# Products of two head pairs in one step, and six parts of w_out streamed from DRAM

## The chip, the core and the metric

The kernel runs on one core of a Trainium2 chip. A core has five engines with queues of their own: TensorE (PE, matrix products; its weight loads are shown as PEld), VectorE (DVE), ScalarE (ACT), GpSimd (POOL) and SyncE (SP), which here issues every DMA. Each works through its instructions in order and waits on semaphores of the others. The metric is the device time of one execution in microseconds; a profiled execution also gives the span from the first to the last instruction.

## What is computed

Eight batches with eight heads of attention over keys and values that are averaged in groups of eight, then a feed-forward layer with a squared ReLU over all 4608 tokens:

```python
B, H, S, D = 8, 8, 576, 64
k_p = k.reshape(B, H, S // 8, 8, D).mean(axis=3)      # 72 pooled keys a head
v_p = v.reshape(B, H, S // 8, 8, D).mean(axis=3)
scores = np.matmul(q, k_p.transpose(0, 1, 3, 2)) / np.sqrt(D)
attn = np.exp(scores - np.max(scores, axis=-1, keepdims=True))
attn = attn / (np.sum(attn, axis=-1, keepdims=True) + 1e-09)
x = np.matmul(attn, v_p).transpose(0, 2, 1, 3).reshape(B * S, H * D)   # 4608 x 512
h = np.maximum(x @ w_in, 0.0)                          # w_in 512 x 2048
out = h * h @ w_out                                    # w_out 2048 x 512
```

All is in float32. From chunk 1 on the two big products are made as three products of a high and a low half (float32r) each: high times high, high times low, low times high.

## The kernel before

The tokens are cut into 12 chunks of 384 (CH); a chunk spans one batch or two. For each chunk the 2048 hidden features are worked in 16 parts of 128 (NFC). One step of the main loop is one (chunk, part): `hidden` makes the part's hidden values on PE into one of two PSUM banks, ACT takes the ReLU, DVE squares it, ACT and DVE split it in a high half gh and a low half gl, and two steps later (LAG) `project` adds its product with that part of w_out to three PSUM banks that stay for the whole chunk. In PE's order a step is: `hidden` of this step, the small products that fall due, `project` of two steps before.

The attention of a chunk is made under the feed-forward layer of the chunk before. It goes by pairs of heads, p = 0 to 3, as stages spread over steps: `turn_q`, `split_q`, `scores`, `exponents`, `send_sums`, `fetch_sums`, `reciprocals`, `fetch_reciprocals`, `weigh_values`. STEADY gives, for chunk 2 on, each pair's first step relative to its chunk's start (-22, -18, -14, -10) and the stages' offsets from it (-1 to 8). So `weigh_values` of pairs 0 to 3 falls in steps -14, -10, -6 and -2, each pair in a step of its own. EARLY is the same for chunk 1, whose stages differ; chunk 0 is made in the prologue.

`weigh_values` (av): for each of the pair's two heads PE multiplies the pooled values vp by the exponents sc; the two heads' results stand in the upper and lower 64 partitions of one PSUM bank of tag "a" (three banks, used by the scores as well). These products are plain float32, of 64 output columns of PE; in the profile each is two passes, and the two heads' passes run side by side. DVE multiplies the bank by the reciprocals rb, ACT copies the high half xh, and DVE subtracts for the low half xl. `hidden` of the chunk reads xh and xl.

The sums over exponents travel through DRAM: SP sends them (rs), fetches them in another shape (rc), DVE takes reciprocals (rr), SP sends those (rd) and fetches them broadcast to all partitions (rb).

The order of all this is fixed by a table: `at(step, f, ...)` enters a stage for a step, and the main loop emits a step's stages in program order on every engine. Loads are collected during a step and issued by SP at its end, behind the small transfers that the stages issue themselves.

Weights stay on the chip. Each of 32 parts (16 of w_in, 16 of w_out) is loaded raw (`land`), unpacked by ACT and DVE (`magnitude`, `to_float32`: tiles wf) and split in two halves (`split_weights`: tiles wt, named w_i and w_o in the profile). All these tiles, and most large tiles of the prologue (values and keys of batches 0 and 1, early exponents te), come from one pool of 4 KB tiles, tag "w", with 2 * NFC + 1 = 33 buffers. A tile gets the buffer of one that has been read for the last time, and its first writer waits for that reader. In the prologue POOL sums the values of batch 1 out of such tiles, heads 0 to 7 in order (`by_halves`; the tile v_1_6 holds heads 6 and 7).

Of the kernel before, what the change touches and what calls it, by code (L numbers as in the profile page):

```python
# [9 lines left out]
F32 = mybir.dt.float32  # L10
F32R = mybir.dt.float32r
# [3 lines left out]
ALU = mybir.AluOpType  # L15
# [22 lines left out]
def pooled_attn_relu2_ffn(  # L38
# [16 lines left out]
    PE, DVE, ACT, GP, SP = (InOrder(tc, e) for e in (nc.tensor, nc.vector, nc.scalar, nc.gpsimd, nc.sync))  # L55
# [4 lines left out]
    P = 128  # L60
    POOL = 8
    SP_ = S // POOL
    NPAIR = H // 2
    NFC = DFF // P
# [4 lines left out]
    NCH = NT // CH  # L69
# [4 lines left out]
    SCALE = 1.0 / (D ** 0.5) / POOL  # L74
    LAG, QL = 2, 5

    IDLE = (10, 3)
    STB, SCB, LD, OB = 1, 2, 4, 3


    FIRST, EAGER, AHEAD = 4, 10, 4
# [2 lines left out]
    SPLIT = 6  # L84


    STEADY = ((-22, -18, -14, -10), (-1, 0, 1, 3, 4, 5, 6, 7, 8))
    KV0 = -39
    EARLY = ((-16, -13, -10, -7), (0, 1, 2, 3, 5))

    NKT = H * SP_ // QT
    KV_AT = (("k", (0, 1, 2, 4, 5, 6), 9, 10, 12), ("v", (9, 10, 12, 13, 15, 16), 19, 20, None))
# [3 lines left out]
    wts = ctx.enter_context(tc.tile_pool(name="wts", bufs=1))  # L96
    sb = ctx.enter_context(tc.tile_pool(name="sb", bufs=2))
    dram = ctx.enter_context(tc.tile_pool(name="dram", bufs=3, space=bass.MemoryType.DRAM))
# [20 lines left out]
    def load(dst, src):  # L119
        loads.append((dst, src))  # L120

    def issue_loads():
        for dst, src in loads:
            dma(dst, src)
        loads.clear()

    def split(hi, lo, src, eng=None):
        ACT.copy(hi, src)
        (eng or DVE).tensor_tensor(lo, src, hi.bitcast(F32), op=ALU.subtract)
# [3 lines left out]
    raw, wf, wt = {}, {}, {}  # L133

    def w_tile(dt, name):
        return wts.tile([P, 2, 512], dt, name=name, tag="w", bufs=2 * NFC + 1)

    halves = {}

    def half_tile(kind, name):  # L140

        if kind not in halves:
            halves[kind] = w_tile(F32, name)
            return halves[kind][:, 0, :]
        return halves.pop(kind)[:, 1, :]
# [37 lines left out]
    def keep_busy(n):  # L183

        for i in range(0, n):
            if i % 8 == 0:
                t = ps_a.tile([P, 512], F32, name=f"idle_{n}_{i}", tag="a")
            PE.matmul(t[:, :P], lhsT=ident, rhs=ident, start=True, stop=True)
# [25 lines left out]
    def pool_k(b, i):  # L214
        if i % KT == 0:
            loaded["kp", b, i // KT] = sb.tile([QT, KT, 2, D], F32, name=f"kp_{b}_{i}", tag="kp", bufs=2)
        kp, kt = loaded["kp", b, i // KT][:, i % KT], loaded.pop(("k", b, i))
        if b == 1:
            by_halves(kp[:, 0, :], kt)
            GP.tensor_tensor(kp[:, 1, :], kt[:, :D], kt[:, D:2 * D], op=ALU.add)  # L220
        else:
            DVE.tensor_reduce(kp[:, 0, :], kt.rearrange("p (o d) -> p d o", d=D), axis=AX.X, op=ALU.add)
            DVE.tensor_copy(kp[:, 1, :], kp[:, 0, :])
# [99 lines left out]
    def segments(c):  # L323
        t, segs = c * CH, []
        while t < (c + 1) * CH:
            b = t // S
            n = min((b + 1) * S, (c + 1) * CH) - t
            segs.append((b, t - c * CH, n))
            t += n
        return segs  # L330
# [191 lines left out]
    def weigh_values(c, p):  # L522

        if p == 0 and c == 0:
            x0.extend(w_tile(F32, f"x_{c}_{i}")[:, :, :CH] for i in range(2))
        elif p == 0:
            xts[c] = (sb.tile([P, NPAIR, CH], F32R, name=f"xh_{c}", tag="xh", bufs=2),
                      sb.tile([P, NPAIR, CH], F32R, name=f"xl_{c}", tag="xl", bufs=2))
        sc, rb = live.pop((c, p))
        av = ps_a.tile([P, 512], F32, name=f"av_{c}_{p}", tag="a")  # L530
        for b, o, n in segments(c):
            for i in range(2):
                PE.matmul(av[i * D:(i + 1) * D, o:o + n], lhsT=kv[b][2][:, 2 * p + i, :], rhs=sc[:, i, o:o + n],
                                 start=True, stop=True)

        def then():
            if c == 0:
                ACT.copy(x0[p // 2][:, p % 2, :], av[:, :CH])
                return
            xh, xl = xts[c]  # L540
            if c == 1:
                split(xh[:, p, :], xl[:, p, :], av[:, :CH])
                return
            DVE.tensor_tensor(rb, av[:, :CH], rb, op=ALU.mult)
            split(xh[:, p, :], xl[:, p, :], rb)

        return then

    gts = {}

# [33 lines left out]
        split(gh, gl, gts[c, fc])  # L584
        gts[c, fc] = (gh, gl)

    accs = {}

    def project(c, fc):
        if fc == 0:  # L590
            accs[c] = [ps_o.tile([P, 512], F32, name=f"o_{c}_{t}", tag=f"o{t}") for t in range(NTT)]
        g, key = gts.pop((c, fc)), ("o", fc)
        for t in range(NTT):
            tt = slice(t * P, (t + 1) * P)
            if c == 0:
                prods = [(g[:, tt], wf[key])]
            else:
                prods = [(g[x][:, tt], wt[key][:, w, :]) for x, w in ((0, 0), (0, 1), (1, 0))]
            for i, (a, w) in enumerate(prods):
                PE.matmul(accs[c][t], lhsT=a, rhs=w, start=fc == 0 and i == 0, stop=fc == NFC - 1 and i == len(prods) - 1)  # L600

        def store():
            for t in range(NTT):
                ob = sb.tile([P, DM], F32, name=f"ob_{c}_{t}", tag="ob", bufs=OB)
                ACT.copy(ob, accs[c][t])
                dma(out[c * CH + t * P:c * CH + (t + 1) * P, :], ob)

        return store if fc == NFC - 1 else None
# [5 lines left out]
    def at(step, f, *a):  # L614
        work.setdefault(max(step, -PRO), []).append((f, a))
# [27 lines left out]
    issue_loads()  # L643
    keep_busy(IDLE[0])
    for i in range(KT + 2):
# [4 lines left out]
    pool_k(0, KT + 2)  # L650
    keep_busy(IDLE[1])
    after = [token_scores(0, 0), transpose_k(0, 1)]
# [15 lines left out]
    for p in range(NPAIR):  # L668
# [4 lines left out]
        if p > 1:  # L673
            keep_busy(IDLE[1])
        if p:
            weigh_values(0, p - 1)()
        if p:
            keep_busy(IDLE[1])
        if p in (1, 2):
# [5 lines left out]
    to_float32(*first_keys[2:])  # L685
    keep_busy(IDLE[1])
    weigh_values(0, NPAIR - 1)()
    keep_busy(IDLE[1])
    for hf in range(2):
# [5 lines left out]
    t = 1e9  # L695
    for key in reversed(keys):
        t = min(t - 1 / RATE, need[key] - 1 - MARGIN)
        need[key] = math.floor(t)
    for i, key in enumerate(keys):
        if i >= EAGER:  # L700
            at(need[key] - AHEAD, land, key)
        if i >= FIRST:
            at(need[key] - 1, magnitude, key)
            at(need[key], to_float32, key)
        if key[0] == "i" and key[1] * WC >= SPLIT * P:
            at(need[key] + 1, split_weights, key, DVE)
        else:
            at(14 + int(i * 0.48), split_weights, key, DVE)


    def kv_steps(b, s):
        for kind, load_at, send_at, fetch_at, turn_at in KV_AT:
            for i in range(NKT):
                at(s + load_at[i], load_rows, kind, b, i)
                at(s + load_at[i] + 2, pool_rows, kind, b, i)
            at(s + send_at, send_rows, kind, b)
            at(s + fetch_at, fetch_rows, kind, b)
            if turn_at:
                at(s + turn_at, turn_k, b)
# [3 lines left out]
    for c in range(1, NCH):  # L723
        first, offsets = EARLY if c == 1 else STEADY
        names = (transpose_q, token_scores, token_normalise, token_turn, weigh_values) if c == 1 else stages
        for b, _, _ in segments(c):
            if b not in ready:
                ready.add(b)
                kv_steps(b, c * NFC + KV0)
        for p in range(NPAIR):  # L730
            s = c * NFC + first[p]
            if c > 1 or p:
                at(s - QL, load_q, c, p)
            for d, f in zip(offsets, names):
                at(s + d, f, c, p)


# [2 lines left out]
    for s in range(-PRO, len(steps) + LAG):  # L740
        todo = work.get(s, [])
        activate = hidden(*steps[s]) if 0 <= s < len(steps) else None
        later = [f(*a) for f, a in sorted(((f, a) for f, a in todo if f in on_pe), key=lambda x: x[0] is weigh_values)]
        store = project(*steps[s - LAG]) if s >= LAG else None
        if 0 <= s - 1 < len(steps):
            split_hidden(*steps[s - 1])
        for f in later:
            f()
        for f, a in todo:
            if f not in on_pe + last:  # L750
                f(*a)
        keys = [a[0] for f, a in todo if f is to_float32]
        if keys:
            to_float32(*keys)
        for f, a in todo:
            if f is split_weights:
                f(*a)
        issue_loads()
        for f in (activate, store):
            if f:  # L760
                f()
# [30 lines left out]
```

## Time and profile before

| | us |
|---|---|
| three runs, median (lowest to highest) | 945.41 (945.24 to 947.99) |
| the profiled execution | 946.16 |
| its span | 944.4 |
| PE busy | 929.4 |
| DVE, ACT, POOL busy | 598.3, 434.4, 352.9 |
| 128x384 products h from xh and from xl, 1488 and 744 | 417.1 and 249.8 |
| 128x512 products o from gh and from gl, 1056 and 528 | 333.9 and 208.8 |
| av products, 256 records | 43.8 |

Every instruction is recorded at line 34, since a helper keeps program order there; so rows are told apart by the tiles' names, out<-in. A row of the timeline has the start in us from the span's beginning, the duration in us, the engine, the operation with its tiles and shape, how many were merged, and in brackets the engine's idle time just before and what ended it. A busy time of PE counts overlapping matmuls once; ends of matmuls are modelled, so distances between starts are the surer measure.

### The profile page before, as it was taken

How to read it: one execution, taken by the hardware profiler on the slowest of the kernel's cores; microseconds unless marked ns; L12 is line 12 of the kernel's file. 1: busy time of each engine (PE TensorE's matmuls, PEld its weight loads, DVE VectorE, ACT ScalarE, POOL GpSimd, SP SyncE). 2: the span in 40 equal slices, each digit the busy share in tenths (PEclk: the TensorE clock that was granted, in tenths of full speed). 3: DMA queues.
4: the chain of work that ended last, by engine and by line, in shares of the span. 5: the costliest groups of instructions: out<-in, count | busy, mean ns of one | idle time of the engine just before them, and what ended most of it. 6: DMA issues, size and time to landing. Idle time of an engine off the chain costs nothing.

```text
span 944.4 us, 13423 instructions
## 1 busy us (share of the span) xinstructions
PE 929.4 (98%) x4776; PEld 785.4 (83%) x4776; DVE 598.3 (63%) x1020; ACT 434.4 (46%) x903; POOL 352.9 (37%) x215
## 2 busy tenths in 40 slices
PE   7899999999999999999999999999999999999998
PEld 6556668888888888888888888888888888888997
DVE  7988896766655576776765576676765555553221
ACT  3888766654434344344435334434434443432222
POOL 3820144435344443534443443435344443530000
PEclk9999999999999999999999999999999999999999
DMA  9975213223112113223211023223311101100000
GB/s 258 319 241 144 73 40 104 60 69 99 43 30 68 36 50 95 68 73 87 63 36 52 19 68 87 51 75 91 70 41 40 53 18 28 50 10 10 34 1 33
DMA packets 124682, 68.06 MB, mean 72 GB/s; under 512 B 95800, under 2 KB 105224, under 8 KB 124616
## 3 DMA queue, kind: packets, MB, share of 16 engines
q1 hardware_dynamic: 124616, 67.22, 26.3%
q8 instruction: 37, 0.61, 0.3%
q14 instruction: 29, 0.24, 0.1%
HBM read 55.73 MB, written 11.45 MB: 71 GB/s over the span
## 4 chain that ended last, share of the span: by engine, by line
PE 88%; DMA 4%; DVE 3%; POOL 2%; ACT 2%; issue 1%; SPq 0%; DVEq 0%; ACTq 0%
PE o L34 41%; PE h L34 40%; PE av L34 3%; PE sps L34 3%; POOL v L34 2%; DMA k<-in_k_dram 1%; DMA v<-in_v_dram 1%; DVE wf_o L34 1%; DVE wf_i L34 1%; POOL vp L34 1%; DMA raw_i<-in_moe_w_in_dram 1%; DMA vv<-in_v_dram 1%; DVE tm L34 1%; ACT te L34 1%; DVE w_i L34 0%
## 5 line engine op out<-in xcount | busy, mean ns | idle before, releaser
L34 PE MATMUL h<-xh,w_i 128*128 128x384 f32 x1488 | 417.1, 341 | 0.0
L34 PE MATMUL o<-w_o,gh 128*128 128x512 f32 x1056 | 333.9, 397 | 0.0
L34 PEld LDWEIGHTS h<-xh,w_i 128*128 128x128 f32 x1488 | 272.6, 188 | 10.7 <-issue 2.2
L34 POOL PARTITION_ALL_REDUCE tot<-sc x80 | 202.2, 2574 | 188.6 <-issue 178.4
L34 PE MATMUL h<-xl,w_i 128*128 128x384 f32 x744 | 249.8, 336 | 0.0
L34 PEld LDWEIGHTS o<-w_o,gh 128*128 128x128 f32 x1056 | 193.1, 188 | 51.6 <-issue 16.5
L34 POOL PARTITION_ALL_REDUCE mx<-sc x80 | 114.8, 1483 | 285.3 <-ACT sc L34 279.3
L34 DVE TENSOR_TENSOR gl<-r,gh 128x384 fp32r<-128x384 f32 x176 | 137.0, 779 | 114.4 <-ACT gh L34 114.4
L34 PE MATMUL o<-w_o,gl 128*128 128x512 f32 x528 | 208.8, 395 | 0.0
L34 DVE TENSOR_TENSOR r<-r 128x384 f32<-128x384 f32 x160 | 100.8, 630 | 132.8 <-ACT r L34 131.0
L34 ACT ACTIVATE r<-h 128x384 f32<-128x384 f32 x192 | 94.4, 492 | 136.0 <-PE h L34 135.0
L34 ACT CAST gh<-r 128x384 fp32r<-128x384 f32 x176 | 90.4, 514 | 130.3 <-DVE r L34 129.8
L34 PEld LDWEIGHTS h<-xl,w_i 128*128 128x128 f32 x744 | 139.7, 188 | 10.6 <-issue 3.1
L34 PEld LDWEIGHTS o<-w_o,gl 128*128 128x128 f32 x528 | 99.1, 188 | 22.2
L34 ACT CAST xh<-rb 128x384 fp32r<-128x384 f32 x40 | 20.5, 513 | 120.2 <-DVE rb L34 120.2
L34 ACT ACTIVATE sc<-sc 72x384 f32<-72x384 f32 x80 | 39.7, 525 | 47.0 <-DVE sc L34 47.0
L34 DVE TENSOR_TENSOR rb<-av,rb 128x384 f32<-128x384 f32 x40 | 22.3, 557 | 40.5 <-PE av L34 40.5
L34 DVE TENSOR_TENSOR st<-qt,st 64x384 fp32r<-64x384 f32 x80 | 44.2, 553 | 3.5 <-ACT st L34 1.0
L34 ACT COPY sc<-sps 72x384 f32<-72x384 f32 x80 | 34.1, 477 | 26.6 <-PE sps L34 26.6
L34 PE MATMUL av<-sc,vp 72*64 72x384 f32 (+1 forms) x256 | 43.8, 426 | 2.3 <-ACT sc L34 2.3
L34 PE MATMUL o<-wf_o,r 128*128 128x512 f32 x96 | 44.6, 601 | 0.0
L34 DVE TENSOR_REDUCE kp<-k 96x64 f32<-96x512 f32 x42 | 43.6, 1038 | 0.1
(82 smaller groups left out, 709.6 us busy)
## 6 DMA issues: line engine op xcount, KB each, us to landing
k<-in_k_dram SPq DMA_DIRECT2D x48, 192.0 KB
out_dram<-ob SPq DMA_DIRECT2D x36, 256.0 KB
raw_i<-in_moe_w_in_dram SPq DMA_DIRECT2D x16, 512.0 KB
raw_o<-in_moe_w_out_dram SPq DMA_DIRECT2D x16, 512.0 KB
rb<-rd SPq DMA_DIRECT2D x80, 96.0 KB
v<-in_v_dram SPq DMA_DIRECT2D x36, 192.0 KB
q<-in_q_dram SPq DMA_DIRECT2D x112, 48.0 KB
q<-in_q_dram SPq DMA_DIRECT2D x96, 24.0 KB
```

The lines of the kernel that those rows point to most:

```text
L34: return lambda *a, **k: self.tc.keep_in_program_order(f(*a, **k))
```

## The change

Three things change.

1. The offset of `weigh_values` becomes 12, 8, 12, 8 for the pairs 0 to 3: from chunk 2 on pairs 0 and 1 both fall in step -10 of their chunk, pairs 2 and 3 in step -2. A third sc buffer (SCB) holds the exponents of the pair that waits longer. The subtractions for xl are put behind both pairs' multiplications and copies (`split_lows`).
2. The pool of tag "w" has 31 buffers instead of 33 (WB).
3. So that this suffices, parts 1, 3, 5, 7, 9 and 11 of w_out don't stay: when such a part has been split, both halves are sent to DRAM (`send_weights`), and for each chunk from 2 on they are fetched six steps (LEAD) ahead of their product (`fetch_weights`, tiles ws) and dropped after it.

```diff
+    WB, FLOW, LEAD = 2 * NFC - 1, range(1, 13, 2), 6
-    STB, SCB, LD, OB = 1, 2, 4, 3
+    STB, SCB, LD, OB = 1, 3, 4, 3
...
-    STEADY = ((-22, -18, -14, -10), (-1, 0, 1, 3, 4, 5, 6, 7, 8))
+    STEADY = ((-22, -18, -14, -10), [(-1, 0, 1, 3, 4, 5, 6, 7, x) for x in (12, 8, 12, 8)])
-    EARLY = ((-16, -13, -10, -7), (0, 1, 2, 3, 5))
+    EARLY = ((-16, -13, -10, -7), [(0, 1, 2, 3, 5)] * NPAIR)
...
-        return wts.tile([P, 2, 512], dt, name=name, tag="w", bufs=2 * NFC + 1)
+        return wts.tile([P, 2, 512], dt, name=name, tag="w", bufs=WB)
...
             DVE.tensor_tensor(rb, av[:, :CH], rb, op=ALU.mult)
-            split(xh[:, p, :], xl[:, p, :], rb)
+            ACT.copy(xh[:, p, :], rb)
+            lows.append((xl[:, p, :], rb, xh[:, p, :]))
...
+    def split_lows():
+        for lo, src, hi in lows:
+            DVE.tensor_tensor(lo, src, hi.bitcast(F32), op=ALU.subtract)
+        lows.clear()
...
+    def send_weights(f):
+        d = scratch[f] = dram.tile([P, 2, 512], F32, name=f"wd_{f}", tag=f"wd_{f}", bufs=1)
+        load(d, wt["o", f].bitcast(F32))
+
+    def fetch_weights(c, f):
+        t = flowing[c, f] = w_tile(F32R, f"ws_{c}_{f}")
+        load(t.bitcast(F32), scratch[f])
...
         g, key = gts.pop((c, fc)), ("o", fc)
+        w_o = wf[key] if c == 0 else flowing.pop((c, fc)) if (c, fc) in flowing else wt[key]
...
-                prods = [(g[x][:, tt], wt[key][:, w, :]) for x, w in ((0, 0), (0, 1), (1, 0))]
+                prods = [(g[x][:, tt], w_o[:, w, :]) for x, w in ((0, 0), (0, 1), (1, 0))]
...
+        if key[0] == "o" and key[1] in FLOW:
+            at(16 + int(i * 0.48), send_weights, key[1])
+            for c in range(2, NCH):
+                at(c * NFC + key[1] + LAG - LEAD, fetch_weights, c, key[1])
...
-            for d, f in zip(offsets, names):
+            for d, f in zip(offsets[p], names):
                 at(s + d, f, c, p)
...
         for f in later:
             f()
+        split_lows()
```

The first place is PE's order in step 22, chunk 1's part 6, where pair 1 of chunk 2 is due (av_2_1; the numbers behind a name are chunk, pair or part, and a running number of the tile). Before:

```order
L34 MATMUL h_1_6_1664<-xl_1_791,w_i_3_2_775 128x384
L34 MATMUL h_1_6_1664<-xh_1_790,w_i_3_2_775 128x384
L34 MATMUL av_2_1_1677<-sc_2_1_1344,vp_1_324 64x384 x2
L34 MATMUL o_1_0_1474<-w_o_4_1561,gh_1_4_1629 128x512 x2
L34 MATMUL o_1_0_1474<-w_o_4_1561,gl_1_4_1630 128x512
```

The same place on PE in the changed kernel:

```order
L34 MATMUL h_1_6_1660<-xl_1_791,w_i_3_2_775 128x384
L34 MATMUL h_1_6_1660<-xh_1_790,w_i_3_2_775 128x384
L34 MATMUL av_2_0_1675<-sc_2_0_1155,vp_1_324 64x384 x2
L34 MATMUL av_2_1_1678<-sc_2_1_1344,vp_1_324 64x384 x2
L34 MATMUL o_1_0_1469<-w_o_4_1555,gh_1_4_1625 128x512 x2
L34 MATMUL o_1_0_1469<-w_o_4_1555,gl_1_4_1626 128x512
```

av of pair 0 has moved here from four steps earlier, behind the same h and directly ahead of pair 1's; where it stood, h is now followed by o.

The second place is ACT's order in step 0, where it writes the exponents te of chunk 1's pair 0. The rows name the semaphores that an instruction waits for. Before:

```order
L34 ACTIVATE r_0_0_587<-h_0_0_549 128x384
L34 ACTIVATE r_0_0_587<-r_0_0_587 128x384 [waits Activation_49]
L34 ACTIVATE te_1_0_606<-sps_1_0_0_595,tm_1_0_605 96x72 [waits DVE_49,PE_49]
L34 ACTIVATE te_1_0_606<-sps_1_0_0_595,tm_1_0_605 96x72 x3
L34 ACTIVATE te_1_0_606<-sps_1_0_1_596,tm_1_0_605 96x72 [waits DVE_49,PE_49]
```

The same place on ACT in the changed kernel:

```order
L34 ACTIVATE r_0_0_587<-h_0_0_549 128x384
L34 ACTIVATE r_0_0_587<-r_0_0_587 128x384 [waits Activation_49]
L34 ACTIVATE te_1_0_606<-sps_1_0_0_595,tm_1_0_605 96x72 [waits DMAHW0_49,DVE_49,DMAHW1_49,PE_49,Pool_49]
L34 ACTIVATE te_1_0_606<-sps_1_0_0_595,tm_1_0_605 96x72 x3
L34 ACTIVATE te_1_0_606<-sps_1_0_1_596,tm_1_0_605 96x72 [waits DVE_49,PE_49]
```

The instructions are the same, but te_1_0 now lies in the buffer of v_1_6, where before it had that of a query tile read long ago; so its first writer also waits for POOL, for the last of its sums over batch 1's values, and for the DMAs that loaded them.

The third place is SP's order in the steps in which pair 1 of chunk 9 sends its sums (rs) and fetches its reciprocals (rb), with w_out's fetches for chunk 8. Before:

```order
L34 DMA rc_9_1_6743<-rs_9_1_6689 96x8
L34 DMA kt_7_6748<-kd_7_6697 32x18x32 x4
L34 DMA v_7_1_6753<-in_v_dram 96x512
L34 DMA rd_9_1_6787<-rr_9_1_6784 96x8
L34 DMA rb_9_1_6820<-rd_9_1_6787 64x384 x2
L34 DMA v_7_2_6838<-in_v_dram 96x512
```

The same place on SP in the changed kernel:

```order
L34 DMA rc_9_1_6826<-rs_9_1_6771 96x8
L34 DMA kt_7_6831<-kd_7_6779 32x18x32 x4
L34 DMA ws_8_7_6825<-wd_7_1792 128x1024
L34 DMA v_7_1_6836<-in_v_dram 96x512
L34 DMA rd_9_1_6871<-rr_9_1_6868 96x8
L34 DMA rb_9_1_6905<-rd_9_1_6871 64x384 x2
L34 DMA ws_8_9_6904<-wd_9_1888 128x1024
L34 DMA v_7_2_6923<-in_v_dram 96x512
```

A fetch of part 7 now stands ahead of pair 1's rd and rb, and one of part 9 right behind them.

More of the change, by code (lines that the diff above doesn't have):

```diff
@@ L544, in then @@
             DVE.tensor_tensor(rb, av[:, :CH], rb, op=ALU.mult)
-            split(xh[:, p, :], xl[:, p, :], rb)
-        return then
+            ACT.copy(xh[:, p, :], rb)
+            lows.append((xl[:, p, :], rb, xh[:, p, :]))
+        return then
+    lows = []
+    def split_lows():
+        for lo, src, hi in lows:
+            DVE.tensor_tensor(lo, src, hi.bitcast(F32), op=ALU.subtract)
+        lows.clear()
     gts = {}
@@ L585, in split_hidden @@
         gts[c, fc] = (gh, gl)
-    accs = {}
+    accs, flowing, scratch = {}, {}, {}
+    def send_weights(f):
[4 more added lines that the diff above has]
+        load(t.bitcast(F32), scratch[f])
     def project(c, fc):
@@ L595, in project @@
             if c == 0:
-                prods = [(g[:, tt], wf[key])]
+                prods = [(g[:, tt], w_o)]
             else:
-                prods = [(g[x][:, tt], wt[key][:, w, :]) for x, w in ((0, 0), (0, 1), (1, 0))]
+                prods = [(g[x][:, tt], w_o[:, w, :]) for x, w in ((0, 0), (0, 1), (1, 0))]
             for i, (a, w) in enumerate(prods):
```

## Prediction

> **What bounds the kernel now.** I read the page from the top: busy time, slices, chain.
>
> ```profile
> span 944.4 us, 13423 instructions
> ...
> PE 929.4 (98%) x4776; PEld 785.4 (83%) x4776; DVE 598.3 (63%) x1020; ACT 434.4 (46%) x903; POOL 352.9 (37%) x215
> ...
> PE   7899999999999999999999999999999999999998
> ...
> PEclk9999999999999999999999999999999999999999
> DMA  9975213223112113223211023223311101100000
> ...
> PE 88%; DMA 4%; DVE 3%; POOL 2%; ACT 2%; issue 1%; SPq 0%; DVEq 0%; ACTq 0%
> ```
>
> TensorE (PE) is busy 98% of the span at full clock and holds 88% of the chain that ended last; only the first two or three slices of 23.6 us show anything else. So there are two regimes, and the windows view separates them: the stretch from PE's last long pause to its next one, and everything from there to the end.
>
> ```profile
> 54.48:104.38 49.90, 49.28 (x244) 31.98 (x245) 41.89 (x91) 43.46 (x100) 0.00 (x0) 1.00 0.65 207
> 112.95:944.40 831.45, 827.78 (x4190) 715.57 (x4188) 501.85 (x817) 353.79 (x726) 313.33 (x158) 1.00 0.21 53
> ```
>
> The first numbers are the length and PE's busy time. From 54.48 us PE lacks 0.62 us in 49.90, from 112.95 us it lacks 3.67 us in 831.45. After about 54 us a microsecond of PE work saved is a microsecond of span, and a microsecond by which PE starts later is one too, because it has no idle time to catch up in.
>
> **The pairing of the products.** These are PE rows of one step with a pair of heads (av) and of a later step without:
>
> ```profile
> 456.39 0.34 PE L34 MATMUL h<-xh,w_i 128*128 128x384 f32 x1
> 456.66 0.87 PE L34 MATMUL av<-sc,vp 72*64 72x384 f32 x4
> 457.45 0.74 PE L34 MATMUL o<-w_o,gh 128*128 128x512 f32 x2
> 458.03 0.39 PE L34 MATMUL o<-w_o,gl 128*128 128x512 f32 x1
> ...
> 466.48 0.33 PE L34 MATMUL h<-xh,w_i 128*128 128x384 f32 x1
> 466.66 0.62 PE L34 MATMUL o<-w_o,gh 128*128 128x512 f32 x2
> 467.11 0.40 PE L34 MATMUL o<-w_o,gl 128*128 128x512 f32 x1
> ```
>
> From the last h to the first gl product passes 458.03 - 456.39 = 1.64 us with av and 467.11 - 466.48 = 0.63 without: a pair costs 1.01 us in a step of its own. Part of that is the way in and out: the first av starts 0.27 us after the last h where o starts 0.18 after it, and the first two o take 0.58 instead of 0.45. What a second pair costs right behind the first is not in this trace as such; the nearest thing is the inside of a block in a chunk that spans two batches (eight passes of 192 columns, two side by side):
>
> ```profile
> 290.48 0.87 PE L34 MATMUL av<-sc,vp 72*64 72x192 f32 x8
> ...
> 290.85 0.49 PE L34 MATMUL av<-sc,vp 72*64 72x192 f32 x4
> ...
> 291.02 0.33 PE L34 MATMUL av<-sc,vp 72*64 72x192 f32 x2
> 291.28 0.50 PE L34 MATMUL o<-w_o,gh 128*128 128x512 f32 x1
> ```
>
> The third couple of passes starts at 290.85, the fourth at 291.02: 0.165 us each (0.17 by the rounded rows), so four couples, one more pair, 0.66 us. In chunks of one batch it is two couples of 384 columns, the same work. I take 0.66, so **each merged step saves 1.01 - 0.66 = 0.35 us**. Chunks 2 to 11 have four pairs each: 40 steps with av become 20 with two, **20 x 0.35 = 7.0 us**. Bounds: the second pair costs at most what the whole block lasts, 457.45 - 456.66 = 0.79 us, a saving of 0.22 x 20 = 4.4; and at least 0.64 (0.16 a couple), 7.4.
>
> **A rule that speaks against it.** The rows of the loads are these:
>
> ```profile
> L34 PEld LDWEIGHTS av<-sc,vp 72*64 72x64 f32 x256 | 14.8, 135 | 16.0 <-issue 11.3 <-ACT sc L34 3.8
> ```
>
> The block above holds eight such loads and lasts 291.28 - 290.48 = 0.80 us, and the block of 456.66, with four, 0.79: the loads lie beside the passes. The Trainium skill (TensorE: Matmul & The Clock Gate, Part 3: Packing small matmuls) says that a weight load overlaps running matmuls only when its row group differs, and here all have the same rows; by that rule the second pair would pay two more loads of 0.135 us, the merge would save 0.08 us, and 20 of them 1.6. The trace of before disagrees with it.
>
> **What hides the rest of the pairing.** VectorE (DVE) and ScalarE (ACT) do the same multiplications, copies and subtractions, but for two pairs in one step. The tightest case is the pair that is needed first, pair 3, two steps ahead of its chunk (chunk 8 here):
>
> ```profile
> 634.78 1.09 SPq L34 DMA_DIRECT2D rb<-rd  x2
> ...
> 641.34 0.87 PE L34 MATMUL av<-sc,vp 72*64 72x384 f32 x4
> 649.22 0.33 PE L34 MATMUL h<-xh,w_i 128*128 128x384 f32 x1
> 651.79 0.40 PE L34 MATMUL o<-w_o,gl 128*128 128x512 f32 x1
> ...
> 642.25 0.56 DVE L34 TENSOR_TENSOR rb<-av,rb 128x384 f32<-128x384 f32 x1 [0.60 <-PE av L34]
> 643.39 0.56 DVE L34 TENSOR_TENSOR xl<-rb,xh 128x384 fp32r<-128x384 f32 x1 [0.58 <-ACT xh L34]
> 646.29 0.56 DVE L34 TENSOR_TENSOR gl<-r,gh 128x384 fp32r<-128x384 f32 x1 [0.58 <-ACT gh L34]
> ```
>
> xl is done at 643.95 and wanted from 649.22: 5.3 us in hand. With two pairs in the step it comes about 0.66 (PE) + 2 x 0.56 (one more rb and xl) = 1.8 us later. Behind it in DVE's order stands gl, the low half of the step's hidden values, done at 646.85 and used at 651.79: 4.9 us in hand for the same 1.8. No PE wait follows; if this cover failed, each microsecond would count 20 times. Pair 3's (and 1's) reciprocals are fetched one step ahead of the product, as before: rb is issued 7.5 us before its use. The third buffer for sc is what lets pairs 0 and 2 wait four steps longer; the av of a pair gives its PSUM bank back with the rb row, a step ahead of the scores that want it. I price all this at 0.
>
> **The part from DRAM.** Six sends and sixty fetches of 512 KB join SP's queue, about 35 MB more beside 68. The nearest rows are a load of a weight part in the chain, and DMA's slices above, 0 to 3 tenths after the first four:
>
> ```profile
> 56.21 6.32 DMA raw_i<-in_moe_w_in_dram
> ```
>
> At most 6.3 us from issue to landing; a fetch is issued six steps, over 25 us, ahead of its product, into a buffer that was last read some steps before. It follows the rb of its step in the queue and precedes the next step's small transfers by about a step. Price 0; bound above in the third rival. Were it late, PE would wait in the o block.
>
> **Two buffers fewer: a new wait at the start.** The pool of 4 KB tiles shrinks from 33 to 31 from the first instruction on, not from chunk 2 on. So tiles of the prologue get other predecessors. I went through all of them: for each, when the last reader of its new predecessor was done in this trace, against when the tile was first written. Loads of raw weights that now wait longer have room: the latest, raw_o of part 13, waits for te of chunk 1's pair 2, read by PE at 92.22, and is first used here:
>
> ```profile
> 92.22 0.82 PE L34 MATMUL pps<-ident,te 96*72 96x96 f32 x8
> ...
> 113.60 0.68 ACT L34 ACTIVATE wf_o<-raw_o 128x512 f32<-128x512 f32 x1
> ```
>
> 93.04 + 6.32 = 99.4 against 113.60. But one computed tile has no room: te of chunk 1's pair 0, written by ACT, now lies where POOL is still summing the values of batch 1 (heads 6 and 7). Those rows:
>
> ```profile
> 48.56 0.65 POOL L34 TENSOR_TENSOR vp<-v 72x64 f32<-72x64 f32 x1
> ...
> 50.49 3.23 POOL L34 TENSOR_TENSOR vp<-v 72x64 f32<-72x64 f32 x1
> ...
> 50.01 1.78 ACT L34 ACTIVATE te<-sps,tm 96x72 f32<-96x72 f32 x8 [1.63 <-DVE tm L34]
> 53.34 0.71 ACT L34 ACTIVATE raw_i<-raw_i 128x512 uint32<-128x512 uint16 x1
> 53.89 0.53 ACT L34 ACTIVATE r<-h 128x384 f32<-128x384 f32 x1
> ...
> 53.75 0.38 SPq L34 DMA_DIRECT2D raw_i<-in_moe_w_in_dram  x1
> ...
> 50.59 2.74 PE L34 MATMUL o<-wf_o,r 128*128 128x512 f32 x6
> 54.48 2.85 PE L34 MATMUL h<-x,wf_i 128*128 128x384 f32 x8 [1.15 <-ACT r L34]
> ...
> 60.12 1.83 DVE L34 TENSOR_TENSOR xl<-x,xh 128x768 fp32r<-128x768 f32 x2 [1.49 <-ACT xh L34]
> ```
>
> POOL's last sum ends at 53.72, te began at 50.01: ACT will stand **3.7 us** longer. Behind te in its order stand the unpacking of two weight parts and the relu at 53.89, for which PE waits already (1.15 us): h moves from 54.48 to 58.2, and PE's pause from 1.15 to 4.9 us. DVE's xl waits for ACT too, so all three engines are late by the same amount, and the window from 54.48 showed that PE has nothing to make it up with. I take +3.7. Bounds: 0, if POOL is done by 50.0; and 4.9, if the disorder costs PE its old pause once more.
>
> **Sum:** -7.0 + 3.7 = -3.3 us. The profiled execution took 946.16 us (span 944.4, 1.8 around it) and would take 942.9; the median of the three is 945.41, 0.75 below it, so I predict **942.1**, 0.35% faster. With the bounds (saving 4.4 to 7.4, stall 0 to 4.9) the forecast runs from 938.0 to 945.9.
>
> **Rivals.**
> 1. *No stall at the start.* POOL's 3.23 us for a sum that takes 0.65 or less elsewhere may be short when ACT and DVE pause, or the buffer is free earlier. For it: spans on POOL are rough. Against: SP's load that waited for the same tile was let go in this trace only at 53.75 us, the end of that row. Then -7.0: 938.4. Chance 0.13.
> 2. *The change doesn't do what it says:* two pairs in a step don't share the way in and out, because each pair has a PSUM bank of its own or pays its loads. Against: the couples at 0.165 us. Worked from the load row it saves 20 x 0.08 = 1.6, and -1.6 + 3.7 = +2.1: 947.5; the 4.4 of the bound gives 944.7. The first end is also what the Trainium skill's rule gives. Chance 0.14.
> 3. *Slower: the fetches hold up pair 1's reciprocals.* One fetch stands ahead of rd and rb of pair 1 in SP's queue. rb has about 5 us in hand (7.5 less its flight), then DVE waits in order, gl is late, and behind gl's 4.9 us PE stops. That decides from a fetch of some 4.2 + 5 + 4.9 = 14 us; at 16 us it costs 2 us in each of ten chunks, +20 - 3.3: about 962. Against: 6.3 us at a DMA load of 65%, and 21% here. Chance 0.05.
> 4. *A second wait at the start* of the size of the first, in a tile that moved and whose predecessor is late only because of the first wait: -7.0 + 7.4, 945.8. Chance 0.1.
>
> **Chances.** Forecast 0.58, rivals 0.13, 0.14, 0.05, 0.1. A measurement tells 0.3%, 2.8 us, from no change: that is 942.6, which cuts through the forecast; I put seven tenths of it below (the saving is bounded more closely than the stall). Faster 0.58 x 0.7 + 0.13 = 0.54; slower is rival 3 and a little of 2, 0.07; the same, 0.39. The range takes in rival 1 and the nearer part of 2 and 4: 938.0 to 946.3.
>
> **What would show it.** Per step: av blocks of 8 (or 16) records, from the last h to the first gl in 2.30 us, 20 times. At the start: ACT's te with an idle of about 5.3 us ended by POOL's vp, PE's h after it with 4.9 us instead of 1.15; every later block of PE later by 3.7 us until about 160 us, from there earlier by 0.35 a merge. PE should show no idle before o blocks of parts 1, 3, 5, 7, 9, 11. The prediction is wrong if the window from 112.95 shrinks by less than 4 us, if PE idles anew in the steady part, or if h at 54.48 stays where it was.

## The result, and the profile after

| | before | after |
|---|---|---|
| median of the runs, us | 945.33 | 939.53 |
| lowest to highest, us | 945.15 to 947.99 | 938.58 to 941.27 |
| ratio after to before, 95% interval | | 0.9936, 0.9917 to 0.9956 |
| profiled execution, us | 946.16 | 941.27 |
| its span, us | 944.4 | 939.2 |
| half clock between 34 and 46 us, us | 3.41 | 10.24 |

The changed kernel is 0.64% faster, 5.8 us; 942.1 was predicted, and 939.53 lies in the range, though the stall of 3.7 us that the 942.1 counts isn't in this execution. The profiled execution is the slowest of its four, by a stretch of half TensorE clock at the start that is told of below. The page of after, with the rows that answer to those of before (span, busy times, PE, its clock and DMA by slices, the chain):

```profile
span 939.2 us, 13611 instructions
...
PE 924.7 (98%) x4776; PEld 789.8 (84%) x4776; DVE 597.3 (64%) x1020; ACT 435.0 (46%) x903; POOL 349.7 (37%) x215
...
PE   7899999999999999999999999999999999999998
...
PEclk9799999999999999999999999999999999999999
DMA  9973315446224234445324234434514402312200
...
PE 88%; DVE 4%; ACT 3%; DMA 1%; issue 0%; SPq 0%; ACTq 0%; DVEq 0%
```

PE still sets the end, and it is busy for 4.7 us less (929.4 before). DMA is busier from the fifth slice on; that is w_out's parts. The 7 in the second slice of the clock is new.

How much of this is the pairing? The windows view measures it between two landmarks that all kernels have: the first product of h in chunk 1's part 2, before the first merge, and in chunk 11's part 0, behind the last. (The first numbers are the length and PE's busy time.) Before:

```profile
140.18:869.42 729.24, 729.24 (x3729) 633.36 (x3727) 456.83 (x743) 315.48 (x651) 303.39 (x154) 1.00 0.23 56
```

After:

```profile
141.89:863.83 721.94, 721.94 (x3729) 636.20 (x3728) 457.65 (x744) 316.09 (x651) 303.71 (x154) 1.00 0.38 103
```

PE has no idle time at all in either, so this is pure work: 729.24 - 721.94 = **7.30 us in 20 merges, 0.365 each**. The same step of chunk 8 as a timeline of PE in after:

```profile
454.17 0.34 PE L34 MATMUL h<-xh,w_i 128*128 128x384 f32 x1
454.43 1.51 PE L34 MATMUL av<-sc,vp 72*64 72x384 f32 x8
455.87 0.73 PE L34 MATMUL o<-w_o,gh 128*128 128x512 f32 x2
456.44 0.39 PE L34 MATMUL o<-w_o,gl 128*128 128x512 f32 x1
```

Eight passes in one block, 455.87 - 454.43 = 1.44 us where four took 0.79: the second pair costs 0.65. From the last h to the first gl product pass 2.27 us; 2.30 was predicted.

The other 7.30 - 5.2 = 2.1 us of the span went at the ends: the first landmark is 1.71 us later (141.89 against 140.18), and the end takes 0.4 us longer. So the start is where the prediction has to be looked at. Its rows in after (POOL's first and last sum over batch 1's values, ACT's te, PE's h behind it):

```profile
28.07 1.27 POOL L34 TENSOR_TENSOR v<-v 72x256 f32<-72x256 f32 x2
...
48.20 0.65 POOL L34 TENSOR_TENSOR vp<-v 72x64 f32<-72x64 f32 x1
...
51.73 1.78 ACT L34 ACTIVATE te<-sps,tm 96x72 f32<-96x72 f32 x8 [0.54 <-DMA raw_o<-in_moe_w_out_dram]
...
56.18 1.24 PE L34 MATMUL h<-x,wf_i 128*128 128x384 f32 x3
```

POOL is done at 48.85 us, not at 53.72 as in the trace of before, and te, begun at 51.73, doesn't wait for it. The predicted stall isn't there: h follows without a pause, at 56.18 instead of the 58.2 that was predicted, and PE's old pause of 1.15 us has gone too. What made the start late is the clock. Windows of after:

```profile
31.45:34.86 3.41, 2.05 (x13) 1.11 (x11) 3.38 (x8) 2.94 (x5) 3.41 (x2) 1.00 1.01 383
34.86:45.10 10.24, 10.24 (x36) 7.03 (x35) 7.72 (x14) 5.79 (x10) 9.58 (x13) 0.50 1.05 363
45.10:48.52 3.42, 3.42 (x19) 2.33 (x18) 3.42 (x5) 1.73 (x6) 3.14 (x5) 1.00 0.98 299
```

The third number from the end is the granted clock. PE ran at 0.50 for 10.24 us with work waiting, in before for 3.41 us at the same place:

```profile
31.54:34.95 3.41, 2.00 (x11) 0.94 (x9) 3.38 (x8) 2.82 (x5) 3.33 (x2) 1.00 1.04 364
34.95:38.36 3.41, 3.41 (x16) 2.93 (x16) 3.34 (x7) 1.06 (x2) 3.17 (x6) 0.50 1.03 392
38.36:41.77 3.41, 3.41 (x19) 2.24 (x19) 2.40 (x5) 2.46 (x5) 3.25 (x3) 1.00 1.07 360
```

In both, PE was busy for some 60% of the 3.41 us ahead of the drop, with one idle of about 1.4 us in it.

### The profile page after: what moved, and what is told of

Same layout as the page of the kernel before. It is cut to its first block, busy times and chain, and to the rows that moved or that the text cites. A ratio compares the mean times of both kernels' runs of the same rounds, so it can differ in the third digit from the quotient of the medians.

```text
span 939.2 us, 13611 instructions
## 1 busy us (share of the span) xinstructions
PE 924.7 (98%) x4776; PEld 789.8 (84%) x4776; DVE 597.3 (64%) x1020; ACT 435.0 (46%) x903; POOL 349.7 (37%) x215
## 4 chain that ended last, share of the span: by engine, by line
PE 88%; DVE 4%; ACT 3%; DMA 1%; issue 0%; SPq 0%; ACTq 0%; DVEq 0%
PE o L34 41%; PE h L34 40%; PE av L34 4%; PE sps L34 3%; DVE wf_o L34 1%; DVE wf_i L34 1%; ACT te L34 1%; DMA q<-in_q_dram 1%; DVE tm L34 1%; DVE w_i L34 0%; ACT r L34 0%; ACT raw_i L34 0%; ACT wf_i L34 0%; ACT wf_o L34 0%; DVE xl L34 0%
## 5 line engine op out<-in xcount | busy, mean ns | idle before, releaser
L34 PE MATMUL o<-w_o,gh 128*128 128x512 f32 x696 | 219.1, 396 | 0.0
L34 PEld LDWEIGHTS o<-w_o,gh 128*128 128x128 f32 x696 | 128.0, 188 | 30.5 <-issue 10.0
L34 PE MATMUL o<-w_o,gl 128*128 128x512 f32 x348 | 137.8, 396 | 0.0
L34 PE MATMUL o<-ws,gh 128*128 128x512 f32 x360 | 112.5, 393 | 0.0
L34 PEld LDWEIGHTS o<-w_o,gl 128*128 128x128 f32 x348 | 65.3, 188 | 14.4
L34 PEld LDWEIGHTS o<-ws,gh 128*128 128x128 f32 x360 | 66.5, 189 | 11.0
L34 PE MATMUL o<-ws,gl 128*128 128x512 f32 x180 | 71.3, 396 | 0.0
```

The source lines that it names most:

```text
L34: return lambda *a, **k: self.tc.keep_in_program_order(f(*a, **k))
```

## Experiments

Two theories on the missing stall. **A**: the wait of te for POOL is real, but binds only in executions in which POOL ends later than te could start; the trace of before happened to show a late one. **B**: the wait is there and costs its 3.7 us in most executions, and something else made up for it. Beside them stands the question whether the streaming costs anything, and whether more pairs in a step bring more. The kernel before was run beside each group: 945.04, 945.16, 945.38 and 945.0 us. Edits are against the changed kernel where nothing else is said.

### The streamed parts and the 31 buffers alone

```diff
-    STB, SCB, LD, OB = 1, 3, 4, 3
+    STB, SCB, LD, OB = 1, 2, 4, 3
-    STEADY = ((-22, -18, -14, -10), [(-1, 0, 1, 3, 4, 5, 6, 7, x) for x in (12, 8, 12, 8)])
+    STEADY = ((-22, -18, -14, -10), [(-1, 0, 1, 3, 4, 5, 6, 7, x) for x in (8, 8, 8, 8)])
```

> The 31 buffers and the six streamed parts alone: all pairs weighed at offset 8 again, two sc buffers. Theory A (the pairing saves 20 x 0.36 = 7.2 us; streaming and two buffers fewer cost nothing; what the profiled execution of the change lost at its start, 1.7 us, is a longer stretch of half TensorE clock that comes and goes): 945.3, like before, within 1. Theory B (as predicted: ACT's te of chunk 1 waits for POOL): 949.0, PE's h of step 3 at 58.2 us. Theory C (the fetches lengthen something in the steady part): over 947 with PE idle ahead of o blocks.

Measured: 947.23 us, ratio 1.0017 (1.0004 to 1.0031), some 2 us slower than before, and between the 945.3 of its theory A and the 949.0 of B. The windows view clears the streaming at once; from landmark to landmark stream_only has

```profile
143.70:872.94 729.24, 729.24 (x3728) 633.38 (x3727) 457.35 (x743) 315.44 (x651) 303.50 (x154) 1.00 0.37 102
```

729.24 us as before, with a DMA share of 0.37 instead of 0.23. So the 60 fetches cost nothing and the pairing owns all of the 7.30 us. The loss stands at the start, and here the predicted stall is to be seen (timeline of POOL, ACT and PE in stream_only; this execution, 950.13 us, is the slowest of its ten):

```profile
51.30 0.65 POOL L34 TENSOR_TENSOR vp<-v 72x64 f32<-72x64 f32 x1
...
51.98 1.77 ACT L34 ACTIVATE te<-sps,tm 96x72 f32<-96x72 f32 x8 [4.90 <-POOL vp L34]
...
56.38 2.93 PE L34 MATMUL h<-x,wf_i 128*128 128x384 f32 x4 [4.33 <-ACT r L34]
```

POOL ends at 51.95, te starts at 51.98 after an idle of 4.90 us that POOL ended, PE pauses 4.33 us. And the pause has a sequel that the prediction hadn't priced, in the windows of stream_only:

```profile
52.97:56.38 3.41, 0.00 (x0) 0.00 (x0) 2.92 (x10) 3.38 (x10) 0.00 (x0) 1.00 1.04 329
56.39:59.80 3.41, 3.41 (x6) 1.90 (x7) 2.27 (x4) 3.38 (x7) 0.00 (x0) 0.50 1.05 398
59.81:63.22 3.41, 3.41 (x20) 2.22 (x19) 0.00 (x0) 2.18 (x6) 0.00 (x0) 1.00 1.03 361
```

PE stood still for 3.41 us and then got half its clock for 3.41 us with work waiting, which costs half of that, 1.7 us, more.

### The same, with a buffer of its own for te

This is stream_only with one more edit:

```diff
-            e = w_tile(F32, f"te_{c}_{p}")[:QT...
+            e = (sb.tile([P, 2, NQ * SP_], F32, name=f"te_{c}_{p}", tag="te", bufs=1) if (c, p) == (1, 0) else w_tile(F32, f"te_{c}_{p}"))[:QT...
```

> The streamed parts and the 31 buffers alone, as in the kernel stream_only (947.23 us), but te of chunk 1's pair 0 has a buffer of its own, so ACT no longer waits for POOL's last sum over v_1. Theory A (the whole loss of stream_only, 947.23 - 945.04 = 2.2 us, is that wait and the half clock behind it; the streaming itself costs nothing): about 945.0, the kernel before, between 944.5 and 945.6; in the trace te starts about 50 us, ended by DVE's tm and not by POOL, PE's pause ahead of h of step 3 is about 1.1 us instead of 4.34, and no half clock follows it. Theory B (the transfers of w_out's parts cost the 2.2 us somewhere in the steady part): 947.2 still.

Measured: 945.62 us, ratio 1.0006 (0.9997 to 1.0015), at the upper end of A's range. In the trace te doesn't wait for POOL:

```profile
50.72 1.77 ACT L34 ACTIVATE te<-sps,tm 96x72 f32<-96x72 f32 x8 [0.87 <-DVE tm L34]
...
55.19 2.85 PE L34 MATMUL h<-x,wf_i 128*128 128x384 f32 x8 [0.39 <-ACT r L34]
```

te is released by DVE, and the pause is 0.39 us with no half clock behind it. But POOL was done at 49.51 here, ahead of te, so the shared buffer wouldn't have held te in this execution either. The medians differ by 1.6 us and nine of the twelve runs lie below all ten of stream_only, while the intervals of the two ratios overlap. That points to the wait and doesn't prove it; the pair of kernels with POOL's sum made five times, below, does.

### The change with one streamed part, with more dummies, and once more

The first has 32 buffers and streams part 1 alone; the second adds four dummy products to PE at each of two places of the prologue (`keep_busy`), meant to keep the clock up; the third is the changed kernel again.

```diff
-    WB, FLOW, LEAD = 2 * NFC - 1, range(1, 13, 2), 6
+    WB, FLOW, LEAD = 2 * NFC, (1,), 6
```

```diff
         if p > 1:
-            keep_busy(IDLE[1])
+            keep_busy(IDLE[1] + 4)
```

> The pairing with 32 buffers and one streamed part (part 1) instead of 31 and six. Theory A: the same as the full change, 938.2 to 939.5; 19 or 20 blocks of two pairs at 1.44 to 1.45 us. Theory C (streaming takes back some of the gain): faster than the full change by a us or more, about 937. Theory B: as the full change, since te of chunk 1 still waits for POOL here.

> The full change with four dummy products more ahead of av of chunk 0's pairs 1 and 2 (about 1.0 us each, where PE idled 1.1 and 1.4 us). If the half-clock stretch from 34.9 us follows from PE's pauses ahead of it, no or a shorter stretch of half clock shows, h of step 0 starts at 41 us or earlier and the time is 937 to 938, with less spread. If the stretch has another cause, the clock stays at half from 34.9 us and the time is that of the full change or up to 2 us more.

> The full change once more, for a second profile of its start. Theory A: PE's h of step 0 between 41 and 43 us, later only by what the granted clock explains; the time 938 to 941 by it; POOL's last sum of batch 1's values done ahead of ACT's te. Theory B: te held by POOL, h of step 3 at 58 us.

Measured: 940.53 (ratio 0.994, 0.9924 to 0.9956), 938.71 (0.9935, 0.9913 to 0.9957), 938.71 (0.9923, 0.9906 to 0.994): their intervals overlap. The first is a us above the 938.2 to 939.5 that was expected, so theory C, that one part alone is faster, finds no support. None of their three traces has a te that waits for POOL. Those of the first two have 10.24 us of half clock at about 21 us, the first another 3.41 us at 38 us; change_again has 3.41 us at 34 us, where the changed kernel's first trace had 10.24. So the length of that stretch isn't a property of the kernel. The dummies missed what they were expected to do: PE's h of step 0 starts at 43.12 us, not by 41. Nothing stands at 34.9 us with them, but whether they moved the stretch is open, as pair_one_part has it at the same place without them. In change_again the start reads

```profile
48.05 0.65 POOL L34 TENSOR_TENSOR vp<-v 72x64 f32<-72x64 f32 x1
...
49.25 1.77 ACT L34 ACTIVATE te<-sps,tm 96x72 f32<-96x72 f32 x8 [1.39 <-DVE tm L34]
...
53.70 2.85 PE L34 MATMUL h<-x,wf_i 128*128 128x384 f32 x8 [0.88 <-ACT r L34]
```

POOL ends at 48.70, half a microsecond ahead of te. That is close, so the next two kernels push POOL over that edge.

### POOL's last sum made five times, without and with a buffer of its own for te

```diff
-        GP.tensor_tensor(dst, src[:, :D], src[:, D:2 * D], op=ALU.add)
+        for _ in range(n_last):
+            GP.tensor_tensor(dst, src[:, :D], src[:, D:2 * D], op=ALU.add)
...
-            by_halves(vp, vt)
+            by_halves(vp, vt, 5 if h == 7 else 1)
```

> The changed kernel with POOL's last sum over v_1 made five times instead of once; te of chunk 1's pair 0 still lies in the buffer that POOL reads. Four more sums of 0.65 us are 2.6 us: POOL ends near 51.3 us instead of 48.7. Theory A (the wait is real, but binds only if POOL ends later than te could start, 49.25 us in change_again): te starts at 51.3, its idle is ended by POOL, h of step 3 comes 4.4 us behind POOL's end as in stream_only (51.95 to 56.38), 55.7 instead of 53.7; the median is 938.7 + 2.0 = 940.7, up to 942.4 if a half clock stretch (1.7 us) follows PE's pause. Theory B (the wait costs nothing at any time, because ACT makes it up): 938.7 within 0.5.

> The same five sums on POOL, but te of chunk 1's pair 0 has a buffer of its own. Theory A (it is the wait on that buffer and nothing else that POOL's lateness costs): 938.7 within 0.5, te's idle ended by DVE's tm, and late_sums longer by 2.0 or more. Theory B: the same as late_sums. Rival C (POOL's longer work costs DVE or ACT time at the start even without the wait): both are late by about the same 1 to 2 us.

Measured: late_sums 943.07 us (ratio 0.9971, 0.996 to 0.9982), late_sums_own_te 938.91 (0.993, 0.9918 to 0.9942). The same POOL work costs 4.2 us with the shared buffer and nothing that these runs can tell with a buffer of te's own. The rows of late_sums:

```profile
49.47 3.14 POOL L34 TENSOR_TENSOR vp<-v 72x64 f32<-72x64 f32 x5
...
52.65 1.77 ACT L34 ACTIVATE te<-sps,tm 96x72 f32<-96x72 f32 x8 [4.76 <-POOL vp L34]
...
57.04 2.29 PE L34 MATMUL h<-x,wf_i 128*128 128x384 f32 x3 [4.18 <-ACT r L34]
```

and of late_sums_own_te:

```profile
49.32 3.14 POOL L34 TENSOR_TENSOR vp<-v 72x64 f32<-72x64 f32 x5
...
48.84 1.77 ACT L34 ACTIVATE te<-sps,tm 96x72 f32<-96x72 f32 x8 [1.16 <-DVE tm L34]
```

POOL ends at 52.6 and 52.5 in them; in the one te waits for it, in the other te has begun 3.6 us before. Theory A holds and B falls: the wait is real, it isn't made up, and it binds when POOL ends later than te could start. The loss was larger than the 2.0 to 3.7 us that A expected: 4.2 by the medians. In late_sums half clock sets in 1.6 us before PE's pause ends (55.42 against 57.04) and lasts 6.83 us, twice the stretch of stream_only:

```profile
55.42:62.25 6.83, 5.21 (x8) 2.71 (x9) 3.90 (x8) 5.23 (x11) 0.00 (x0) 0.50 0.80 281
```

The changed kernel itself with te in its own buffer (the edit shown for stream_own_te):

> The changed kernel, te of chunk 1's pair 0 in a buffer of its own. Theory A (in the changed kernel POOL is done at 48.7 to 48.9 us, ahead of the moment at which te could start anyway, so the wait seldom binds): 938.7 within 0.6, no different from change_again. Theory B (the predicted stall of 3.7 us is there in most executions that were not profiled): 935.0 to 936.5.

Measured: 938.33 us, ratio 0.9927 (0.9913 to 0.9941), no different from change_again, as A forecast. But A's premise, that POOL is done by 48.9, fails in this very execution:

```profile
49.45 0.49 POOL L34 TENSOR_TENSOR vp<-v 72x64 f32<-72x64 f32 x1
...
48.97 1.77 ACT L34 ACTIVATE te<-sps,tm 96x72 f32<-96x72 f32 x8 [0.69 <-DVE tm L34]
```

POOL ends at 49.94, and te has begun a microsecond before; with the shared buffer it would have had to wait. So what the wait costs the changed kernel differs from execution to execution, and on average it is less than these runs can tell.

### What sets POOL's end

```diff
     def to_float32(*keys):
+        if len(keys) > 1:
+            for key in keys:
+                to_float32(key)
+            return
```

> What sets POOL's end? In the traces each of POOL's sums of 2.79 or 3.23 us over v_1 (0.32 us where nothing runs beside it) begins just ahead of a run of four SCALAR_TENSOR_TENSOR on DVE (wf from raw, 0.68 us each, two weight parts in turns) and ends with the run. Here DVE unpacks one part after the other (TENSOR_SCALAR and two SCALAR_TENSOR_TENSOR, then the next part's), otherwise the changed kernel. Theory A (POOL gets no turn while such DVE instructions follow each other without a gap, so its end depends on where its sums meet them): no sum of vp longer than 1.7 us (two SCALAR_TENSOR_TENSOR, 1.36, and the sum's own 0.32), as a part's chain has a TENSOR_SCALAR and a gap between the runs. Rival (POOL's long sums have another cause, a DMA's writes or POOL's own issue): sums of 2.79 us or more remain. The time is of no matter: 938.7, within 2 us.

What the expectation speaks of, in after (timeline of POOL and DVE):

```profile
31.42 2.79 POOL L34 TENSOR_TENSOR vp<-v 72x64 f32<-72x64 f32 x1
41.59 0.32 POOL L34 TENSOR_TENSOR vp<-v 72x64 f32<-72x64 f32 x1
...
31.54 1.28 DVE L34 SCALAR_TENSOR_TENSOR wf_i<-wf_i,raw_i 128x512 uint32<-128x512 uint32 x2
32.75 1.28 DVE L34 SCALAR_TENSOR_TENSOR wf_i<-raw_i,wf_i 128x512 uint32<-128x512 uint32 x2
```

The same sum takes 0.32 us with DVE idle and 2.79 beside these four of DVE's instructions with two inputs, which follow each other; it ends at 34.21, 0.2 us behind the last of them (32.75 + 1.28 = 34.03). The 3.23 us of the prediction's row is such a case as well: it ends at 53.72, DVE's run beside it at 53.54. With DVE taking one weight part after the other, the first and the last sum of the longest length in one_key_at_a_time are

```profile
32.00 0.65 POOL L34 TENSOR_TENSOR vp<-v 72x64 f32<-72x64 f32 x1
...
46.53 0.65 POOL L34 TENSOR_TENSOR vp<-v 72x64 f32<-72x64 f32 x1
```

All eight sums lie between 0.32 and 0.65, and POOL needs 47.18 - 28.67 = 18.5 us for them and the v steps between them, where after needs 20.8 and before 24.3. No sum is longer than the 1.7 us that theory A allowed, and the long sums of the rival are gone. But A's wording, that POOL gets no turn beside such a run, is too strong. A later run of four in after lets POOL through:

```profile
45.87 1.94 DVE L34 SCALAR_TENSOR_TENSOR wf_o<-wf_o,raw_o 128x512 uint32<-128x512 uint32 x2
47.73 1.67 DVE L34 SCALAR_TENSOR_TENSOR wf_o<-raw_o,wf_o 128x512 uint32<-128x512 uint32 x2
```

These four take 3.53 us (45.87 to 49.40) where the four above take 2.49, and POOL's sum at 48.20, in the midst of them, takes 0.65. So one time POOL pays and another time DVE; what decides between them isn't shown. The time was a miss: 944.85 us (ratio 0.9989, 0.9973 to 1.0005) instead of 938.7 within 2. DVE's unpacking is slower in this order (0.81 us from start to start of a part's two such instructions beside POOL's sums and 0.73 without, against 0.60 with two parts in turns). In the trace steps 9 to 12 take 2.9 us more than in after, and 3.41 us of half clock stand there. How much of the miss comes from either wasn't tested.

### Four pairs in one step

All four pairs of a chunk three steps ahead of it; pair 3's stages begin a step earlier.

```diff
-    WB, FLOW, LEAD = 2 * NFC - 1, range(1, 13, 2), 6
+    WB, FLOW, LEAD = 2 * NFC - 2, range(1, 15, 2), 6
-    STB, SCB, LD, OB = 1, 3, 4, 3
+    STB, SCB, LD, OB = 1, 5, 4, 3
-    STEADY = ((-22, -18, -14, -10), [(-1, 0, 1, 3, 4, 5, 6, 7, x) for x in (12, 8, 12, 8)])
+    STEADY = ((-22, -18, -14, -11), [(-1, 0, 1, 3, 4, 5, 6, 7, x) for x in (19, 15, 11, 8)])
...
-        rb = sb.tile([P, CH], F32, name=f"rb_{c}_{p}", tag="rb", bufs=2)
+        rb = sb.tile([P, CH], F32, name=f"rb_{c}_{p}", tag="rb", bufs=4)
...
-        for lo, src, hi in lows:
+        for lo, src, hi in lows[:2]:
             DVE.tensor_tensor(lo, src, hi.bitcast(F32), op=ALU.subtract)
-        lows.clear()
+        del lows[:2]
```

> A version that could beat both kernels: the products of all four pairs of a chunk in one step, three steps ahead of it (so pair 3's stages begin a step earlier); five sc and four rb buffers, seven streamed parts, 30 buffers in the pool, and the low halves of two pairs put off by a step. Instead of 20 merged switches there are 30 (four steps with av become one in each of ten chunks): 10 x 0.355 = 3.6 us less than the changed kernel, 938.7 - 3.6 = 935.1; here te of chunk 1's pair 0 doesn't wait for POOL, which would show only where that wait bound. Rival (DVE's cover fails: four multiplications and then low halves ahead of gl make PE wait for gl or xl): each 0.36 us of such a wait in each of ten chunks gives the gain back, 938.7 or more, and PE's idle ahead of o or h in the steps -2 to 0 of a chunk would show it.

Measured: 941.63 us, ratio 0.9958 (0.9945 to 0.997), slower than change_again by 2.9. The cover failed, but neither for xl nor for gl. DVE in the second step ahead of chunk 3, and PE in the one behind it:

```profile
272.82 1.91 DVE L34 TENSOR_TENSOR gl<-r,gh 128x384 fp32r<-128x384 f32 x1 [0.58 <-ACT gh L34]
274.66 1.01 DVE L34 TENSOR_TENSOR xl<-rb,xh 128x384 fp32r<-128x384 f32 x2
275.70 1.14 DVE L34 TENSOR_TENSOR st<-qt,st 64x384 fp32r<-64x384 f32 x2
...
276.40 0.28 PE L34 MATMUL sps<-st,kl 128*72 128x192 f32 x1 [0.39 <-DVE st L34]
276.98 0.28 PE L34 MATMUL sps<-st,kl 128*72 128x192 f32 x1 [0.21 <-DVE st L34]
```

Two xl stand ahead of st, and PE waits for st twice. xl itself isn't wanted until 279.64, so the next kernel puts `split_lows` behind the step's other stages:

```diff
-        split_lows()
         for f, a in todo:
             if f not in on_pe + last:
                 f(*a)
+        split_lows()
```

> four_pairs (941.63 us) with one edit: the subtractions for xl stand behind a step's other stages on DVE instead of ahead of them. In four_pairs PE waited for DVE's st (low halves of a query tile) before the scores of the step ahead of a chunk: the two xl (1.02 us) stood ahead of st in DVE's order, and that step's h-to-h distance was 5.90 us where the changed kernel has 4.92; 0.82 to 0.99 us in each of nine chunks, some 8 us. Theory A (that wait is the whole loss): 941.63 - 8 = 933.6, and by the other way 938.7 - 10 x 0.355 = 935.2; between 933.4 and 935.6; no step distance is longer than the changed kernel's but for the four-pair step itself (+2.93). Rival (the four pairs stretch another wait, for xl or gl, that stood hidden behind it): above 936.5, with PE's idle ahead of h in a chunk's first step.

Measured: **934.01 us, ratio 0.9879 (0.9864 to 0.9894), faster than both kernels.** The same place of DVE, and between the landmarks:

```profile
271.26 1.14 DVE L34 TENSOR_TENSOR st<-qt,st 64x384 fp32r<-64x384 f32 x2
272.43 1.03 DVE L34 TENSOR_TENSOR xl<-rb,xh 128x384 fp32r<-128x384 f32 x2
```

```profile
138.00:857.34 719.34, 719.22 (x3729) 637.13 (x3727) 467.23 (x744) 311.04 (x651) 305.80 (x154) 1.00 0.40 110
```

719.34 against 729.24 of before: 9.90 us for 30 merged switches; 30 x 0.365 would be 10.95. The distances from a step's first product of h to the next step's show where the missing 1 us is. Most of it, 0.88 us, lies in four steps (part 15 of chunks 3, 4, 6 and 7) that take 0.22 us longer than in after. In the first of them DVE's second st is ready at 345.99 us, and PE's product from it starts 0.37 us behind the one before it, where 0.17 is usual. So st is still a little late there, which the expectation ruled out. And of the 4.7 us by which the median is below that of change_again, only 721.94 - 719.34 = 2.60 lie between the landmarks. The rest lies outside them, mostly at the start: te begins at 47.86 in this trace while POOL goes on to 53.29, so it doesn't wait for POOL, and no half clock stands ahead of the first landmark.

## Why the prediction came out as it did

**What bounds the kernel: right.** Between the landmarks PE's busy time equals the length to the hundredth, before and after.

**The pairing: right.** 7.0 us were forecast from a second pair at 0.66 us; measured are 7.30 in all and 0.65 for the second pair. The inside of a block in the trace of before was the right row to price it by. The Trainium skill's rule (TensorE: Matmul & The Clock Gate, Part 3: Packing small matmuls), by which only 1.6 us would have been saved, is not borne out here as the prediction applied it: four more passes with two more pairs of loads took 0.65 us, and four pairs in a row (30 merges) went on saving. That the merge and nothing else made the 7.30 is shown by stream_only, which has all the rest of the change and 729.24.

**The streaming at 0 and the two-pair cover at 0: right**, by stream_only's 729.24 and by PE's lack of idle time in after. The cover's working looked at xl and gl only; with four pairs the first to give way was st, which no term had named.

**The stall: the step that failed**, "POOL's last sum ends at 53.72, te began at 50.01: ACT will stand 3.7 us longer". Its mechanism is right, as stream_only and late_sums show: te is held by POOL, PE's pause grows to 4.33 us (4.9 was forecast) and is never won back. Wrong was to take both ends of the margin from one execution as the kernel's own. POOL's end is one: 53.72 in the trace of before, 51.95 in stream_only, but 48.85 and 48.70 in the two traces of the change, ahead of te at 51.73 and 49.25. Its sums began 1.4 us later in before than in after (29.44 against 28.07), and three runs of DVE's instructions held it there, two in after. The moment at which te could start is the other end, and it moves with TensorE's clock, as te needs PE's products sps. Where POOL doesn't hold te, te begins at 50.8 to 52.7 in the traces with 10.24 us of half clock ahead of it, and at 47.9 to 50.0 in those with 3.41 us or none (at 50.72 in the one with two stretches of 3.41 us). In after te began 2.9 us behind POOL's end, in change_again 0.55 us; that neither shows the wait is in part luck. So the first rival, no stall, with 938.4, described the kernel best, and it had a chance of 0.13. What the prediction held against it, that a load was let go only at 53.75, was true of that execution and said nothing of others. That 939.53 still lies in the range is owed to the range's lower end, which allowed for a stall of 0. By the prediction's own sign, an idle of te that POOL's vp ends, the stall is absent from both traces of the change. Nor did the step price the half clock around such a pause, 1.7 us or more in the two traces in which the wait binds.

**The sum.** The profiled pair: -7.30, +1.71 at the first landmark, +0.4 at the end make -5.2 of span. By medians the change gains 5.8 (6.3 in the second comparison) of the 7.30. The rest, about 1 us, lies in the start, whose clock differs from execution to execution; how it is shared between that and a wait that sometimes binds is open: te's own buffer brought 0.4 us, less than these runs can tell. Open too is why the wait seems to cost stream_only more, 1.6 us by the medians of it and stream_own_te, though up to the first landmark it differs from the changed kernel by the third sc buffer alone.

## What to carry to other kernels

When small products of one kind interrupt a stream of large ones, price the way in and out apart from the products: what is inside a block of the trace shows the price of one more in the same block. When a pool shrinks, list the tiles that get a new predecessor; a margin between two engines that is read from one execution is only as firm as the time at which either comes there, so look in the same trace for how much one and the same instruction varies, and if it does, give the tile a buffer of its own. Before work is piled into one step, walk through everything behind it in that engine's order, not only the tiles that the work makes.

## What was not expected of the hardware

- POOL's sum of 72x64 elements took from 0.31 to 3.23 us in these traces, by what DVE did beside it; the experiment with one part at a time cut the longest to 0.65. The Trainium skill says that GpSimd shares its SBUF interfaces with VectorE, with contention for DVE instructions with two SBUF inputs (GPSIMD Engine Reference, 8. Key points). This agrees. The traces show besides that a small sum can be held for a whole run of four of them, and that in other runs of four POOL gets its turns and DVE's instructions take up to 1.22 us instead of 0.68.
- Half clock came in stretches of 3.41, 6.83 and 10.24 us, one to three times the window of 3413 ns that the Trainium skill gives (TensorE: Matmul & The Clock Gate, Part 1: The HAM clock gate). In that part's table half clock follows an idle window; here it also came after windows in which PE was busy for 60%, with one idle of 1.4 us, and at the same place it lasted 3.41 us in one execution of the changed kernel and 10.24 in another.
